# Window attention on one Trainium2 core: the table of offloaded score tiles planned anew, with no score tile computed twice

## The chip, the core and the metric

The kernel runs on one core of one Trainium2 chip. The core's engines run side by side and are tied together by semaphores: TensorE (PE, matmuls, with its weight loads shown apart as PEld), VectorE (DVE), ScalarE (ACT), GpSimd (POOL) and SyncE (SP, which here only issues DMAs). The metric is the device time of one execution in microseconds (us). Matmul results land in PSUM, which the program divides into eight banks of 512 fp32 columns on 128 partitions; everything else of the working set lies in SBUF.

## The reference

An image of 224 x 224 positions with 96 channels (bf16) goes through cross-shaped window attention. Half of the channels attend inside horizontal stripes of 8 rows, the other half inside vertical stripes of 8 columns; a stripe has 8 x 224 = 1792 tokens, and there are 28 stripes of each direction.

```python
sw = 8; C2 = C // 2; nh, nw = H // sw, W // sw
qkv = einsum('bhwc,cd->bhwd', x, wqkv)
q, k, v = qkv[..., :C], qkv[..., C:2*C], qkv[..., 2*C:]
scale = C2 ** -0.5
# first 48 channels: stripes of 8 rows
qh, kh, vh = [t[..., :C2].reshape(B*nh, sw*W, C2) for t in (q, k, v)]
ah = softmax(einsum('bqc,bkc->bqk', qh, kh) * scale)
oh = einsum('bqk,bkc->bqc', ah, vh)
# last 48 channels: the same over stripes of 8 columns -> ov
o = concat(oh, ov)                      # per position
return einsum('bhwd,dc->bhwc', o, wo)
```

So each of the 56 stripes has a softmax over a 1792 x 1792 score matrix, and the exponentials of all of these, 56 x 1792 x 1792 = 180 million, are most of the elementwise work.

## The kernel before, in words

**Tiles.** Stripes go in 28 pairs P (14 pairs of row stripes, then 14 of column stripes); the two stripes of a pair sit in the two halves of the partitions. A pair's 1792 queries are cut into four chunks c of 512, 512, 512 and 256. A score tile is a key block of 128 keys against one chunk of 512 queries for both stripes: 128 partitions x 1024 fp32, two PSUM banks. (In the 256 chunk a tile takes two key blocks.) This gives 14 + 14 + 14 + 7 = 49 tiles a pair and 1372 in all.

**What happens to a tile.** PE computes the scores, an exponential is taken of all 128 x 1024, the result is written as bf16 into one of 16 buffers `PT`, and PE multiplies it with V (`pv_fn`, L696) into an accumulator bank. A row of ones in V gives the softmax's denominator. There are two kinds of tile:

- Kind "A": the scores (`qk_fn`, L670) go into bank pair 0/1, 2/3 or, when it is free, 6/7. ScalarE reads them there and takes the exponential (L888, one ACTIVATE a tile).
- Kind "P", off ScalarE: the scores (`s_fn`, L683, with one row more in the contraction, which adds a constant so that the bits of the fp32 word can be read as a power of two) always go into banks 6/7 (`PB0`). The exponential is built out of those bits: the upper half of the word gives the power of two, a parabola of the lower half corrects it. Three ways of doing this are in the code, and which one a tile takes is decided when its first VectorE step is planned:

```python
tl["whole"] = backlog(t) < 2.0 * how()[11]                                # L1189
tl["stay"] = not tl["whole"] and backlog(t) >= 2.0 * how()[12]             # L1190
```

`backlog` is the planned time of the work that waits for GpSimd, in us. The three ways are:

1. *Copied* (`whole`): VectorE copies the whole tile to a buffer `qb` (L1191) and the banks are free; GpSimd does the rest in four steps (L1108 to L1111).
2. *Made twice* (neither): VectorE takes the lower halves out with one pass (L1192) and the banks are free; GpSimd squares them (L1105); then PE computes the same scores again into banks 6/7 (a second `s_fn`), and VectorE joins both with one pass (L1213).
3. *Stays* (`stay`): VectorE does three passes (L1192, L1205, L1213) while the scores stay in banks 6/7.

**The planner.** The order of every engine's instructions is fixed when the program is built. A list scheduler (`Sched`, `step_pe`, `step_dve`, `step_pool`) steps through planned time with durations written in the file (L25 to L40) and takes for each engine the next piece of work; `settle` and `emit` then write each engine's stream with the semaphore waits. What the planner may choose is set by the table `HOW`, one row for each pair:

- a string of three digits: how many of the tiles of chunks 0, 1 and 2 are of kind "P" (`OFF`, L73; chunk 3 has none),
- `TAIL`: how late the next pair's projections are spread,
- four rules of 13 digits, one for each chunk (`RULES`, L75). Digits 0 to 5 are thresholds for when PE goes over to PV matmuls, how many tiles off ScalarE may be under way, and which bank is kept; 6 an order on VectorE; 7 whether kind "A" may use banks 6/7; 8 and 10 small time windows; 9 whether the last sum of an output group goes to GpSimd (L584) or stays on VectorE (L593); 11 and 12 the two thresholds quoted above.

**Around it.** PE also runs the projections of the next pairs (K L435 with eviction L440, Q L435 with L451, V L481 with L488) and the output projections (L530, L566, with L537, L545, L573, L580, L593), in four banks 4 to 7 that they share with the PV accumulators and the "P" tiles. Columns and transposes come by DMA from the SP queue. When the share of PE's matmuls in the last 3.4 us falls, the planner puts small matmuls on a buffer of zeros in (L1095). Each engine works strictly in the order of its stream.

Of the kernel before, what the change touches and what calls it, by code (L numbers as in the profile page):

```python
# [40 lines left out]


HOW = [
    ("013", 9, "4551280019333 2571180019333 2583180019323 4583180019323"),
    ("434", 9, "4583180029333 3994191014411 2642191020314 2642191020310"),
    ("444", 2, "2642191020241 2642191020242 2622191020232 2682191020233"),
    ("433", 2, "2682191020434 2682171020430 2682171005430 3682171035430"),
    ("334", 8, "3733151007440 3734151007442 5983170025134 3351190004341"),
    ("444", 9, "3353190009341 3353190009341 3212271001233 3212271101433"),
    ("433", 6, "3212271101433 3213171101433 3213171121433 4144251027212"),  # L50
    ("254", 6, "3982170130134 2191161009232 3774280007321 5774280007321"),
    ("323", 6, "3933181026442 5933181026242 5993181026242 5993181026242"),
    ("443", 7, "5993160026242 5913160025242 5913160025442 5613160025443"),
    ("344", 9, "3a73180118424 3a73180118440 3a73180138440 3a73181138440"),
    ("434", 2, "3a73181138420 3a73181034420 3a44360007332 2464141207431"),
    ("333", 12, "3994240136212 3943290210143 4583180234434 4724171025341"),
    ("433", 12, "4771171035341 3422181006331 4482181006331 4482181016331"),
    ("333", 8, "5024381000243 3021381030243 2832290100230 4743281017314"),
    ("444", 0, "4743250017314 2334371013432 2331371023432 2733371023422"),
    ("413", 8, "2731371023420 2731271023440 2731271023414 2732271020424"),  # L60
    ("444", 6, "3611271029414 3611271029434 3612271019434 3612271019432"),
    ("323", 10, "2a83291022413 2a83291002413 2a83291006443 2a83271006443"),
    ("345", 9, "2a83271036443 3a83271036443 5871260114024 2942340018221"),
    ("334", 1, "2942371018224 2942361018224 2474291006112 2474291006124"),
    ("333", 1, "2444291006444 2044291026444 3884140034313 3884290034313"),
    ("333", 9, "3884290024313 3881290024313 2183281019241 2183281239341"),
    ("434", 7, "4733270022423 4733270022423 4733151022423 4783151022433"),
    ("333", 5, "5443191025313 5643191125213 5644191025213 5434190106422"),
    ("444", 6, "2163161034424 2183161034424 2583161004421 2983161004420"),
    ("432", 2, "5844290117302 5844290117312 5844290127314 2844290127340"),  # L70
    ("444", 12, "2844290125340 2844290110340 3792181100323 3212370220212"),
]
OFF = [[int(d) for d in k] + [0] for k, _, _ in HOW]  # L73
TAIL = [t for _, t, _ in HOW]
# [1287 lines left out]
```

## Time and profile before

Three runs took 1017.83 us in the median (1017.16 to 1017.92). The profiled execution took 1017.39 us, with a span of 1015.6 us from its first to its last instruction.

| | busy, us | share of the span | instructions |
|---|---|---|---|
| PE (matmul) | 979.1 | 96% | 13404 |
| PEld (weight loads) | 394.3 | 39% | 13404 |
| DVE | 959.7 | 94% | 1517 |
| ACT | 1004.8 | 99% | 1101 |
| POOL | 921.6 | 91% | 702 |

In rows of groups the columns are line, engine, operation, output <- inputs with shapes and count; then busy time in us, the mean of one in ns; then the idle time of that engine just before such instructions, and who ended it. The mean of one can be longer than its share of the busy time, because instructions of an engine overlap at their ends. Of the 1372 tiles ScalarE took 1090 and the other 282 went the three other ways: 136 copied (the count of L1191), 75 staying (that of L1205) and 71 made twice (that of L1105). The second scores of those 71 are in L683's count: 4 x (282 + 71) = 1412.

### The profile page before, as it was taken

The numbers are of one execution on the slowest core, as the hardware profiler recorded it, in microseconds if no ns is written. First come the engines' busy times: TensorE is split into PE (matmuls) and PEld (weight loads), VectorE is DVE, ScalarE is ACT, GpSimd is POOL, SyncE is SP. The second block draws the span as 40 slices with busy tenths as digits, with TensorE's granted clock in tenths as the row PEclk, the third lists the DMA queues.
The fourth block names the chain that finished last, engine by engine and source line by source line (L and its number), as shares of the span: only waits on it lengthen the run. The fifth ranks groups of instructions, "written<-read, shape, count | busy, mean of one in ns | idle before, by whom it ended". The sixth has DMA issues, their size and how long they took to land.

```text
span 1015.6 us, 30858 instructions
## 1 busy us (share of the span) xinstructions
PE 979.1 (96%) x13404; PEld 394.3 (39%) x13404; DVE 959.7 (94%) x1517; ACT 1004.8 (99%) x1101; POOL 921.6 (91%) x702
## 2 busy tenths in 40 slices
PE   9999999999999999999999999999999999999998
PEld 4433433343343333334333433434343333443333
DVE  7999999999999999999999999999999999999997
ACT  8999999999999999999999999999999999999997
POOL 4988999999988999989999999989989999998895
PEclk9999999999999999999999999999999999999999
DMA  4402112303220311211022033213313321221111
GB/s 87 98 29 65 38 42 66 65 2 79 65 38 29 79 38 30 65 38 39 2 39 50 19 65 62 49 23 64 48 25 60 57 43 36 58 54 22 25 26 34
DMA packets 162875, 47.04 MB, mean 46 GB/s; under 512 B 155895, under 2 KB 162711, under 8 KB 162738
## 3 DMA queue, kind: packets, MB, share of 16 engines
q1 hardware_dynamic: 161906, 44.62, 21.8%
q8 instruction: 105, 1.72, 0.7%
q10 hardware_dynamic: 832, 0.44, 0.2%
q14 instruction: 32, 0.26, 0.1%
HBM read 10.60 MB, written 19.28 MB: 29 GB/s over the span
## 4 chain that ended last, share of the span: by engine, by line
ACT 97%; PE 2%; DVE 1%; issue 0%; DVEq 0%; ACTq 0%
ACT PT L888 97%; PE ps L696 0%; PE ps L346 0%; PE ps L670 0%; DVE out_all L593 0%; DVE PT L1213 0%; ACT xT_sb L747 0%; PE ps L731 0%; PE ps L566 0%; DVE rc L573 0%; DVE OT_sb L1166 0%; PE ps L481 0%; DVE warm L309 0%; PE ps L683 0%; DVEq L192 0%
## 5 line engine op out<-in xcount | busy, mean ns | idle before, releaser
L888 ACT ACTIVATE PT<-ps 128x1024 bf16<-128x1024 f32 x1090 | 1000.4, 1092 | 1.2 <-PE ps L670 1.1
L670 PE MATMUL ps<-QT_sb,KT_sb 49*64 49x512 bf16 (+1 forms) x5144 | 447.7, 363 | 28.5 <-ACT PT L888 12.4
L696 PE MATMUL ps<-PT,V_sb 128*49 128x512 bf16 (+1 forms) x3136 | 456.2, 361 | 0.7 <-ACT PT L888 0.5
L670 PEld LDWEIGHTS ps<-QT_sb,KT_sb 49*64 49x64 bf16 x5144 | 130.1, 103 | 366.9 <-ACT PT L888 351.0
L1109 POOL TENSOR_TENSOR PT<-PT 128x1024 f16<-128x1024 f16 x136 | 257.6, 1894 | 10.1
L696 PEld LDWEIGHTS ps<-PT,V_sb 128*49 128x49 bf16 x3136 | 133.9, 103 | 165.2 <-issue 129.4
L1110 POOL TENSOR_SCALAR qb<-PT 128x1024 uint16<-128x1024 f16 x136 | 183.7, 1350 | 11.8
L1192 DVE TENSOR_SCALAR qb<-ps 128x1024 f32<-128x1024 uint16 x146 | 178.3, 1221 | 7.5 <-PE ps L683 5.8
L1213 DVE SCALAR_TENSOR_TENSOR PT<-ps,PT 128x1024 uint16<-128x1024 bf16 x146 | 178.0, 1219 | 4.2 <-PE ps L683 3.7
L1108 POOL TENSOR_SCALAR PT<-qb 128x1024 f16<-128x1024 uint16 x136 | 142.4, 1047 | 41.7 <-DVE qb L1191 32.1
L1191 DVE COPY qb<-ps 128x1024 f32<-128x1024 f32 x136 | 166.2, 1222 | 8.6 <-PE ps L683 7.1
L1111 POOL TENSOR_SCALAR PT<-qb 128x1024 uint16<-128x1024 f32 x136 | 142.4, 1047 | 11.0
L683 PE MATMUL ps<-QT_sb,KT_sb 50*64 50x512 bf16 x1412 | 139.5, 385 | 1.9 <-DVE PT L1213 0.4
L1105 POOL TENSOR_TENSOR PT<-qb 128x1024 f16<-128x1024 f32 x71 | 133.1, 1894 | 1.1 <-DVE qb L1192 0.3
L1205 DVE SCALAR_TENSOR_TENSOR PT<-ps,qb 128x1024 f16<-128x1024 uint16 x75 | 91.4, 1219 | 0.2
L1166 DVE CAST OT_sb<-ps 113x512 bf16<-113x512 f32 x112 | 69.3, 619 | 7.1 <-PE ps L696 5.7
L451 DVE CAST QT_sb<-ps 128x512 bf16<-128x512 f32 (+1 forms) x111 | 68.0, 616 | 5.7 <-PE ps L435 5.1
L440 DVE TENSOR_SCALAR_CACHE_REDUCE KT_sb<-ps 128x512 bf16<-128x512 f32 x108 | 66.5, 616 | 1.0 <-PE ps L435 0.7
L584 POOL TENSOR_TENSOR out_all<-tmp,Ph_sb 128x480 bf16<-128x480 f32 (+1 forms) x57 | 59.2, 1046 | 2.6 <-DVE tmp L580 1.4
L488 DVE CAST V_sb<-ps 128x480 bf16<-128x480 f32 (+1 forms) x84 | 52.0, 621 | 4.6 <-PE ps L481 4.3
L545 DVE TENSOR_TENSOR Ph_sb<-ps,rc 128x480 bf16<-128x480 f32 (+1 forms) x84 | 52.2, 621 | 2.0
L683 PEld LDWEIGHTS ps<-QT_sb,KT_sb 50*64 50x64 bf16 x1412 | 40.1, 103 | 34.5 <-DVE PT L1213 13.0
(64 smaller groups left out, 458.1 us busy)
## 6 DMA issues: line engine op xcount, KB each, us to landing
cols_dram<-in_x_dram SPq DMA_DIRECT2D x28, 336.0 KB
out_dram<-out_all SPq DMA_DIRECT2D x388, 24.0 KB, 1.9
xT_sb<-cols_dram SPq DMA_TRANSPOSE x28, 4.7
xT_sb<-in_x_dram SPq DMA_TRANSPOSE x26, 4.5
xT_sb<-ones_dram SPq DMA_DIRECT2D x26, 7.0 KB
Ph_sb<-in_x_dram SPq DMA_DIRECT2D x2, 168.0 KB, 3.5
Ph_sb<-in_x_dram ACTq DMA_DIRECT2D x2, 168.0 KB, 3.7
out_dram<-out_all ACTq DMA_DIRECT2D x4, 24.0 KB, 2.4
```

The lines of the kernel that those rows point to most:

```text
L670: ins = e.matmul(bank(SETS[s] + w)[64 * kh:64 * kh + 64, i * t["qs"]:(i + 1) * t["qs"]], lhsT=KT_sb[b][64 * w:64 * w + CA, kt * 128 + 64 * ...
L683: ins = e.matmul(bank(PB0 + w)[64 * kh:64 * kh + 64, 0:512], lhsT=KT_sb[b][64 * w:64 * w + nr, kt * 128 + 64 * kh:kt * 128 + 64 * kh + 64] ...
L696: ins = e.matmul(bank(pb)[64 * w:64 * w + CA, 0:t["qs"]], lhsT=V_sb[b][:, w, kt, :], rhs=PT[slot][:, ca:ca + t["qs"]], start=st and i == 0 ...
L888: S.commit("act", 0.0, D_ACT, None, lambda e, s=s, slot=slot: e.activation(PT[slot][:], ps[:, 512 * SETS[s]:512 * SETS[s] + 1024], ACTF.Ex ...
L1105: return [("pool", (D_SQ, L_SQ, 0.0), lambda e: e.tensor_tensor(y, q, q, ALU.mult), qk, yk)]
L1108: return [("pool", (D_TS, L_TS, LATE_TS), lambda e: e.tensor_scalar(y, lo, 2.0 ** -16, QH, ALU.mult, ALU.add), qk, yk), ("pool", (D_SQ, L_ ...
L1109: ("pool", (D_SQ, L_SQ, 0.0), lambda e: e.tensor_tensor(y, y, y, ALU.mult), yk + ["pser"], yk),
L1110: ("pool", (D_TW, L_TW, LATE_TS), lambda e: e.tensor_scalar(lo, y, 65536.0 * P2, 65536.0 * QC0, ALU.mult, ALU.add), yk + ["pser"], [("q", ...
L1111: ("pool", (D_TS, L_TS, LATE_TS), lambda e: e.tensor_scalar(bits, q, 1.0, 128.0 * (127.0 - SOFF), ALU.mult, ALU.add), qk, yk)]
L1191: S.commit("dve", t, D_P1, D_P1 + SEMD, lambda e: e.tensor_copy(qb[tl["qb"]][:], ps[:, PB0 * 512:(PB0 + 2) * 512]) if tl["whole"] else e.t ...
L1192: qb[tl["qb"]][:], ps[:, PB0 * 512:(PB0 + 2) * 512]) if tl["whole"] else e.tensor_scalar(
L1213: S.commit("dve", t, D_P1, D_P1 + SEMD, lambda e: e.scalar_tensor_tensor(PT[tl["slot"]][:].bitcast(U16), half(BF16, 1), 128.0 * (127.0 - S ...
```

## The change

Nothing but the table `HOW` is changed: every one of its 28 rows is new, so the number of offloaded tiles of each chunk, `TAIL` and all rules differ. The digit 12 of all 112 rules is now 0. As `backlog(t) >= 0` always holds, a tile that isn't copied stays; the way "made twice" stays in the code and is never taken. The table's off counts add up to 279, where they were 282. Announced split: 163 tiles are copied and 116 stay. The code that computes anything, the buffers, the planner and its durations are the same.

```diff
 HOW = [
-    ("013", 9, "4551280019333 2571180019333 2583180019323 4583180019323"),
-    ("434", 9, "4583180029333 3994191014411 2642191020314 2642191020310"),
...
-    ("432", 2, "5844290117302 5844290117312 5844290127314 2844290127340"),
-    ("444", 12, "2844290125340 2844290110340 3792181100323 3212370220212"),
+    ("022", 8, "4551131003130 2833380005450 2833370015440 2832370011440"),
+    ("444", 7, "2162370010440 2163370010440 2163370010440 2163270010440"),
...
+    ("333", 9, "5931160006230 5223291027430 5223291107430 5223291107430"),
+    ("534", 1, "5722351122030 5782351122030 4993250020220 4993250020220"),
 ]
```

Tiles off ScalarE by pair, 0 to 27, before: 4 11 12 10 10 12 10 11 8 11 11 11 9 10 9 12 8 12 8 12 10 9 9 11 9 12 9 12; and in the new table: 4 12 11 9 10 10 12 10 10 9 11 12 10 10 9 9 11 10 10 9 10 9 9 13 9 10 9 12. Averaged over the 112 rules, digit 11 (the threshold for copying) goes from 2.68 to 3.16, digit 9 from 4.79 to 5.26, digit 10 from 3.13 to 2.73 and digit 5 (tiles under way) from 7.51 to 7.09.

More of the change, by code (lines that the diff above doesn't have):

```diff
@@ L43 @@
 HOW = [
-    ("013", 9, "4551280019333 2571180019333 2583180019323 4583180019323"),
-    ("434", 9, "4583180029333 3994191014411 2642191020314 2642191020310"),
[L46 to L69, printed above, removed]
-    ("432", 2, "5844290117302 5844290117312 5844290127314 2844290127340"),
-    ("444", 12, "2844290125340 2844290110340 3792181100323 3212370220212"),
+    ("022", 8, "4551131003130 2833380005450 2833370015440 2832370011440"),
@@ new lines @@
+    ("444", 7, "2162370010440 2163370010440 2163370010440 2163270010440"),
+    ("344", 12, "2163270010450 2153270010450 3742381018120 3742381028220"),
+    ("333", 1, "2892291134440 2a92291104430 2a22291004430 2a22291014430"),
+    ("334", 9, "2313191038430 2313191038430 4653171020440 4653171000440"),
+    ("433", 9, "4a22241012350 4822261012350 4822261012330 4822261032340"),
+    ("444", 11, "2224270005340 2224370005140 3033181007130 3a33181007330"),
+    ("433", 2, "2934171033250 2931271033250 3033160105350 3033160106350"),
@@ new lines @@
+    ("334", 9, "2572151019130 2572291019130 2372291019330 2372291019030"),
+    ("333", 12, "2371291029030 2371291029030 3792161110340 5763170007410"),
+    ("434", 4, "5763170037430 5a63170037430 5a63170037430 5643160008050"),
+    ("444", 0, "5643160008150 5643160008130 5643160028130 5653160028110"),
+    ("433", 8, "5112140007230 5114140007230 2923160020440 2922160020440"),
+    ("334", 6, "2661370005430 2722271127130 2722271127130 2522171127130"),
+    ("333", 8, "3522171127130 3522171127130 3522171127110 3522271129410"),
@@ new lines @@
+    ("333", 9, "3822271128450 3812271128450 5684350205140 5951190007310"),
+    ("425", 7, "5951190107310 5953190107310 5953190107330 5953190007330"),
+    ("334", 10, "5953191007350 5953191007350 5463170017440 5963170017410"),
+    ("433", 5, "5963170017430 5964170037430 3182261023420 3182241023220"),
+    ("333", 10, "5424270006030 5424270006430 5424270036420 5324270036450"),
+    ("334", 8, "2324270036450 2324270036430 3984371107420 3164160014320"),
+    ("423", 9, "3134160014320 3634160014320 3034160014320 3034160034320"),
@@ L72 @@
+    ("333", 12, "3034160014320 2641381022310 2322281028440 2322280008440"),
+    ("445", 11, "4752391029120 4752290029120 4752290029120 3881151000120"),
+    ("333", 3, "3381151000440 3443191017330 3443191017330 3443190016330"),
+    ("352", 6, "3443190003330 2354360207140 3611281023230 5421360006420"),
+    ("333", 9, "5931160006230 5223291027430 5223291107430 5223291107430"),
+    ("534", 1, "5722351122030 5782351122030 4993250020220 4993250020220"),
 ]
```

## The prediction

> **What bounds the kernel now.** I read the page first: busy time of each engine, then the chain of work that ended last.
>
> ```profile
> span 1015.6 us, 30858 instructions
> PE 979.1 (96%) x13404; PEld 394.3 (39%) x13404; DVE 959.7 (94%) x1517; ACT 1004.8 (99%) x1101; POOL 921.6 (91%) x702
> ACT 97%; PE 2%; DVE 1%; issue 0%; DVEq 0%; ACTq 0%
> ```
>
> Four engines are above 90%, so busy shares alone don't name the bound; the chain does, with 97% on ScalarE. To see whether ScalarE ever rests, the view of busy time by stretches of 100 us (busy and count for PE, PEld, DVE, ACT, POOL, then TensorE clock, DMA share, GB/s) is next:
>
> ```profile
> 9.00:109.00 100.00, 97.13 (x1323) 38.42 (x1321) 94.82 (x144) 99.69 (x109) 81.21 (x63) 1.00 0.26 58
> 209.00:309.00 100.00, 97.30 (x1365) 38.92 (x1362) 97.05 (x143) 100.00 (x110) 91.62 (x68) 1.00 0.23 54
> 809.00:909.00 100.00, 97.51 (x1380) 39.97 (x1376) 94.14 (x159) 100.00 (x110) 95.53 (x70) 1.00 0.24 44
> sum 1000.00, PE 968.83 PEld 387.82 DVE 953.51 ACT 999.61 POOL 916.37; mean PE 96.88 PEld 38.78 DVE 95.35 ACT 99.96 POOL 91.64
> ```
>
> From 9 to 1009 us ScalarE is busy 999.61 of 1000 us. Nothing that makes another engine lighter can shorten this part; only fewer tiles on ScalarE can. The timeline of ScalarE gives the price of a tile (start, length of the merged run, count):
>
> ```profile
> 9.31 21.19 ACT L888 ACTIVATE PT<-ps 128x1024 bf16<-128x1024 f32 x23 [1.10 <-PE ps L670]
> 89.14 81.73 ACT L888 ACTIVATE PT<-ps 128x1024 bf16<-128x1024 f32 x89
> 1008.67 1.15 ACT L888 ACTIVATE PT<-ps 128x1024 bf16<-128x1024 f32 x1
> ```
>
> and the groups by line give counts and durations (busy us, mean ns):
>
> ```profile
> L888 ACT ACTIVATE PT<-ps 128x1024 bf16<-128x1024 f32 x1090 | 1000.4, 1092 | 1.2 <-PE ps L670 1.1
> L670 PE MATMUL ps<-QT_sb,KT_sb 49*64 49x512 bf16 (+1 forms) x5144 | 447.7, 363 | 28.5 <-ACT PT L888 12.4
> L683 PE MATMUL ps<-QT_sb,KT_sb 50*64 50x512 bf16 x1412 | 139.5, 385 | 1.9 <-DVE PT L1213 0.4
> L1191 DVE COPY qb<-ps 128x1024 f32<-128x1024 f32 x136 | 166.2, 1222 | 8.6 <-PE ps L683 7.1
> L1192 DVE TENSOR_SCALAR qb<-ps 128x1024 f32<-128x1024 uint16 x146 | 178.3, 1221 | 7.5 <-PE ps L683 5.8
> L1205 DVE SCALAR_TENSOR_TENSOR PT<-ps,qb 128x1024 f16<-128x1024 uint16 x75 | 91.4, 1219 | 0.2
> L1213 DVE SCALAR_TENSOR_TENSOR PT<-ps,PT 128x1024 uint16<-128x1024 bf16 x146 | 178.0, 1219 | 4.2 <-PE ps L683 3.7
> L1105 POOL TENSOR_TENSOR PT<-qb 128x1024 f16<-128x1024 f32 x71 | 133.1, 1894 | 1.1 <-DVE qb L1192 0.3
> L1108 POOL TENSOR_SCALAR PT<-qb 128x1024 f16<-128x1024 uint16 x136 | 142.4, 1047 | 41.7 <-DVE qb L1191 32.1 <-DVE rc L573 0.5
> L1109 POOL TENSOR_TENSOR PT<-PT 128x1024 f16<-128x1024 f16 x136 | 257.6, 1894 | 10.1
> L1110 POOL TENSOR_SCALAR qb<-PT 128x1024 uint16<-128x1024 f16 x136 | 183.7, 1350 | 11.8
> L1111 POOL TENSOR_SCALAR PT<-qb 128x1024 uint16<-128x1024 f32 x136 | 142.4, 1047 | 11.0
> L584 POOL TENSOR_TENSOR out_all<-tmp,Ph_sb 128x480 bf16<-128x480 f32 (+1 forms) x57 | 59.2, 1046 | 2.6 <-DVE tmp L580 1.4
> ```
>
> The run of 89 tiles is one without a stall: (81.73 - 1.09) / 88 = 0.9164 us a tile, the 1.09 being the mean length of the last. At this pace 1090 tiles take 1089 x 0.9164 + 1.15 = 999.1 us; in fact they go from 9.31 to 1008.67 + 1.15 = 1009.82, that is 1000.5. So all stalls of ScalarE between its first and its last tile come to 1.4 us, each so short that the overlap of neighbouring tiles hides most of it from the busy time. The span is a head of 9.3, 999.1 of tiles, 1.4 of stalls and a tail of 1015.6 - 1009.8 = 5.8 us.
>
> **The change part by part.** *ScalarE, +2.75 us on the path.* The table's counts add up to 279 tiles off ScalarE where they were 282, so L888 goes from 1090 to 1093: 3 x 0.9164 = 2.75. No other work covers it, since ScalarE has no rest to put it into.
>
> *TensorE, off the path.* Score tiles into banks 6/7 were 282 + 71 = 353, at four matmuls each the 1412 of L683. Now they are 279, that is 1116 matmuls: 296 fewer. L670 gets 3 x 4 = 12 more. At 139.5 / 1412 = 0.099 us each the 284 are 28.1 us of busy time. I take nothing for it: the waits by engine show what TensorE does with time that it has over.
>
> ```profile
> PEld ps L670 <- ACT PT L888: 351.0, 926, 0.8
> PEld ps L683 <- DVE PT L1213: 13.0, 50, 0.6
> POOL PT L1108 <- DVE qb L1191: 32.1, 21, 8.4
> ACT PT L888 <- PE ps L670: 1.1, 1, 1.1
> ```
>
> The weight loads of ScalarE's score tiles wait 926 times, 351 us in all, for ScalarE to free its banks, and the one wait of ScalarE for TensorE that is listed is that before its first tile. What TensorE saves lengthens the 351.
>
> *VectorE, +9.8 us.* Copies L1191 from 136 to 163: 27 x 1.222 = +33.0. L1192 from 146 to 116: 30 x 1.221 = -36.6. L1205 from 75 to 116: 41 x 1.219 = +50.0. L1213 from 146 to 116: -36.6. Busy time goes from 959.7 to 969.5, which is 95.2% of a span of 1018.4.
>
> *GpSimd, +9.6 us.* Four steps of a copied tile are 1.047 + 1.894 + 1.350 + 1.047 = 5.338; 27 x 5.338 = +144.1. The 71 squares of L1105 go: 71 x 1.894 = -134.5. From 921.6 to 931.2, 91.4%. Digit 9 may also move some sums of output groups to or from L584, at 1.05 us each; the direction of three or so would be hidden in this, and I cost it at nothing.
>
> Neither sum is on the path while ScalarE is fed: the cover is ScalarE's own 1002 us, and it is gone only where VectorE or GpSimd has no room in some stretch. VectorE was busy 97.05 of 100 us in one stretch above, and GpSimd 95.53 in another, with ScalarE at 100.00 in both; the new means of 95.2 and 91.4 lie under these.
>
> *Banks 6/7.* A tile made twice had the pair twice, each time for one pass of VectorE; a tile that stays has it once for three, 1.221 + 2 x 1.219 = 3.66 us and more if VectorE does other work between. What is queued behind it on those banks is the next offloaded tile and the projections' fills that use banks 6 and 7, and behind these on TensorE, whose stream is in order, the scores for ScalarE. This is where the new order could cost ScalarE something. The holding in sum is the 9.8 us more on VectorE, less the latency of 74 fills.
>
> *Stalls, 1.4 us before.* The trace can't show those of a new order. From below: none at all, -1.4. From above: VectorE can't be filled beyond its present 959.7 / 1015.6 = 94.5%, so that 969.5 takes 1025.9, +7.5 beyond the three tiles. The rows are much nearer to the lower end (the stretch with VectorE at 97.05% has ScalarE at 100.00). I scale the present stalls with VectorE's idle time, from 55.9 to 48.9: 1.4 x 55.9 / 48.9 = 1.6, so +0.2.
>
> *Head and tail, 0.* What runs before the first tile is written by hand, with no digit of the table in it. The end of the chain of waits:
>
> ```profile
> 1009.88 0.42 PE ps L696 x4
> 1010.32 0.44 DVE OT_sb L1166
> 1010.80 0.29 PE ps L566 x8
> 1011.12 0.24 DVE rc L573 x2
> 1011.87 0.45 DVE out_all L593 x2
> ```
>
> These follow ScalarE's last tile, one after the other, whatever the table says: PV, eviction, output projection, reciprocals, scaling, and the last DMA. VectorE work that the new order leaves for the end could stand ahead of them (one pass, +1.2), and a gap or two may close (-0.5).
>
> DMAs, their queues and their number stay; the moments at which SP issues them move with the order, with nothing on ScalarE's path waiting for them (no DMA among its waits).
>
> *Sum.* 9.3 + (1092 x 0.9164 + 1.15 = 1001.9) + 1.6 + 5.8 = 1018.6, against 1015.6: +2.95. The profiled execution took 1017.39, so its like would take 1020.3; the median of the runs, 1017.83, lies 0.44 above it, which gives **1020.8 us**, 0.29% slower. 0.2%, or 2.04 us, is about what a measurement of this kernel can tell from no change.
>
> [...]
>
> ```profile
> L1109 POOL TENSOR_TENSOR PT<-PT x136: 1891/1894/1896, 19.9 to 994.0; 128x1024 f16<-128x1024 f16 x136
> ```
>
> 136 instances within 5 ns of one another, though VectorE was busy 94% of the time and copied 136 times. [...]
>
> **The rivals.**
>
> *TensorE was the bound, faster.* The page has it busy 96%, and 284 matmuls at 0.099 us go: 1017.8 - 28.1 = 989.7. Against it: the 351 us of waits for ScalarE, and 1093 tiles at 0.9164 alone need 1001.7. It decides only if ScalarE's pace depended on TensorE's load, and the pace is the same to within a few ns over all ten stretches (109 or 110 tiles in each). [...]
>
> *The stalls go, no change.* A stall of ScalarE comes where TensorE is late with its scores; the chain shows such a place, between the two runs
>
> ```profile
> 9.31 443.52 ACT PT L888 x483
> 457.48 541.35 ACT PT L888 x590
> ```
>
> where for 4.6 us it goes over TensorE's matmuls. If 74 tiles less for TensorE end all of the 1.4, it is 1017.83 + 2.75 - 1.4 = 1019.2, within 0.2%. It decides when at least 0.7 of the 1.4 go (below 1019.87). For it: stalls are TensorE's, and TensorE gets lighter. Against: TensorE is late mostly because something ahead of it in its order waits for VectorE, and that gets heavier.
>
> *VectorE or GpSimd runs out of room, slower by more.* A stay of 3.66 us in banks 6/7 delays the fills behind it, or a stretch with many copies is late with its `PT`. By the share of 94.5% above: 1017.8 + 10.3 = 1028.1; a third of these stalls gives 1023.1. By GpSimd, 931.2 / 0.9075 is 1026.1 in span, the same. It decides when a stretch asks VectorE for more than the 97% seen. For it: 41 more stays, and GpSimd waits 32.1 us for copies already. Against: the means above.
>
> [...]
>
> *The split isn't 163 and 116.* The total of 279 is fixed by the table; each tile moved from copied to staying costs VectorE 2.44 and saves GpSimd 5.34, which ends in the third rival.
>
> **How the numbers follow.** Forecast (stalls of 0.8 to 3, 1020 to 1022.2): 0.62. Stalls go: 0.17. Out of room or another split: 0.17. TensorE the bound, or a faster ScalarE for a reason that I don't see: 0.03. Locking: 0.01. So faster 0.03; same 0.17 and a little of the forecast's lower edge, 0.19; slower 0.78. The range goes from 1018.9, which leaves out the faster cases and some of the second (stalls gone and a shorter tail), to 1024.2, which takes in the third up to stalls of 5 us.
>
> **What the new profile would show.** L888 x1093 with 1003 us busy, and ScalarE at 99.9 of 100 us in the stretches; no L1105; L1191 x163; L1192, L1205 and L1213 x116; L683 x1116; DVE near 969.5, POOL near 931; the wait of L670's weight loads for ScalarE above 351. The prediction is wrong if ScalarE shows idle time before L888 of several us, if its first tile isn't at 9.3, or if more than 6 us or less than 5 follow its last.

## The result, and the profile after

The changed kernel took 1019.99 us in the median of 12 runs (1019.26 to 1021.12), the kernel before 1017.52 in 12 runs beside them (1016.52 to 1018.35). The ratio is 1.0025 with a 95% interval of 1.0017 to 1.0033: 2.5 us slower. The forecast was 1020.8, with 1018.9 to 1024.2 as its range. The profiled execution took 1019.99, with a span of 1018.2; that of before had 1017.39 and 1015.6, so both rose by 2.6.

The page's first part, and the chain of work that ended last:

```profile
span 1018.2 us, 30267 instructions
PE 964.7 (95%) x13117; PEld 385.9 (38%) x13117; DVE 964.2 (95%) x1534; ACT 1007.7 (99%) x1104; POOL 931.6 (91%) x736
ACT 82%; POOL 13%; PE 3%; DVE 1%; issue 1%; DVEq 0%
```

The groups by line (busy us, mean ns, then idle time before them):

```profile
L888 ACT ACTIVATE PT<-ps 128x1024 bf16<-128x1024 f32 x1093 | 1003.3, 1096 | 1.5 <-PE ps L670 1.3
L1109 POOL TENSOR_TENSOR PT<-PT 128x1024 f16<-128x1024 f16 x163 | 308.8, 1894 | 12.6
L1110 POOL TENSOR_SCALAR qb<-PT 128x1024 uint16<-128x1024 f16 x163 | 220.1, 1350 | 14.2
L1191 DVE COPY qb<-ps 128x1024 f32<-128x1024 f32 x163 | 199.2, 1222 | 12.2 <-PE ps L683 10.5
L1108 POOL TENSOR_SCALAR PT<-qb 128x1024 f16<-128x1024 uint16 x163 | 170.7, 1047 | 30.9 <-DVE qb L1191 17.8
L1111 POOL TENSOR_SCALAR PT<-qb 128x1024 uint16<-128x1024 f32 x163 | 170.7, 1047 | 13.1
L1205 DVE SCALAR_TENSOR_TENSOR PT<-ps,qb 128x1024 f16<-128x1024 uint16 x116 | 141.3, 1218 | 0.1
L683 PE MATMUL ps<-QT_sb,KT_sb 50*64 50x512 bf16 x1116 | 111.2, 387 | 4.2 <-DVE PT L1213 1.9
```

All counts are as announced: 1093 tiles on ScalarE, 163 copied, 116 staying, no L1105, and 1116 score matmuls off ScalarE. What is new is the chain: 13% of it lies on GpSimd, which wasn't in it before. Its pieces in order of time (start, length), at the place where it leaves GpSimd ("issue" is time in which GpSimd waited for nothing that the profile shows; four such pieces of 0.04 to 0.07 us are left out here):

```profile
420.00 1.06 POOL PT L1108
421.13 1.06 POOL PT L1111
422.26 1.90 POOL PT L1109
424.16 0.08 issue
424.24 1.34 POOL qb L1110
425.58 0.08 issue
425.66 1.06 POOL PT L1108
426.79 1.06 POOL PT L1111
427.89 0.83 PE ps L696 x6
428.72 0.37 PE ps L670 x4
```

From 312.4 to 427.9 us the chain stays on GpSimd, which does one copied tile after another without a pause; a tile takes 425.66 - 420.00 = 5.66 us, of which 5.34 is busy and the rest is 0.07 to 0.08 us between the steps. In fact GpSimd has no pause of 0.3 us or more from 18.9 to 534 us; in the kernel before it had ten in that time, 14 us in all. At the end of the stretch PV (L696) waits for the last step, and the scores for ScalarE stand behind PV in TensorE's order. The timelines of TensorE and ScalarE there:

```profile
427.89 0.34 PEld L696 LDWEIGHTS ps<-PT,V_sb 128*49 128x49 bf16 x6 [0.69 <-POOL PT L1111]
429.11 1.94 ACT L888 ACTIVATE PT<-ps 128x1024 bf16<-128x1024 f32 x2 [0.24 <-PE ps L670]
```

This is ScalarE's longest idle time in mid-kernel. There are two more: 0.12 us at 491.0, where a second such stretch of GpSimd in the chain ends (465.3 to 490.2), and 0.06 at 742.5. The end of the kernel, first ScalarE's last piece in the chain and then the last of the tail:

```profile
1004.83 8.26 ACT PT L888 x9
1013.13 0.42 PE ps L696 x4
1013.58 0.44 DVE OT_sb L1166
1015.13 0.45 DVE out_all L593 x2
```

ScalarE's busy time by stretches sums to 999.26 of 1000 us, as good as before:

```profile
sum 1000.00, PE 951.93 PEld 377.99 DVE 955.38 ACT 999.26 POOL 926.32; mean PE 95.19 PEld 37.80 DVE 95.54 ACT 99.93 POOL 92.63
```

ScalarE's last tile ends at 1013.09. Its first starts at 9.31 as before; 1093 tiles at 0.9164 us end at 9.31 + 1092 x 0.9164 + 1.15 = 1011.2, so its stalls came to 1.9 us, and the tail is 1018.2 - 1013.1 = 5.1. Against the kernel before: +2.75 of tiles, +0.5 of stalls, -0.7 of tail, together +2.6 (the first two are counted at the pace of the kernel before, 0.9164).

### The profile page after: what moved, and what is told of

Read it like the earlier page. It is cut to its first block, busy times and chain, and to the rows that moved or that the text cites. A ratio compares the mean times of both kernels' runs of the same rounds, so it can differ in the third digit from the quotient of the medians.

```text
span 1018.2 us, 30267 instructions
## 1 busy us (share of the span) xinstructions
PE 964.7 (95%) x13117; PEld 385.9 (38%) x13117; DVE 964.2 (95%) x1534; ACT 1007.7 (99%) x1104; POOL 931.6 (91%) x736
## 4 chain that ended last, share of the span: by engine, by line
ACT 82%; POOL 13%; PE 3%; DVE 1%; issue 1%; DVEq 0%
ACT PT L888 82%; POOL PT L1109 4%; POOL qb L1110 3%; POOL PT L1108 3%; POOL PT L1111 3%; PE ps L696 1%; PE ps L670 1%; PE ps L346 0%; DVE qb L1192 0%; DVE qb L1191 0%; DVE PT L1205 0%; ACT xT_sb L747 0%; DVE Ph_sb L545 0%; PE ps L731 0%; DVE OT_sb L1166 0%
## 5 line engine op out<-in xcount | busy, mean ns | idle before, releaser
L670 PE MATMUL ps<-QT_sb,KT_sb 49*64 49x512 bf16 (+1 forms) x5156 | 448.5, 363 | 42.7 <-ACT PT L888 29.9
L696 PE MATMUL ps<-PT,V_sb 128*49 128x512 bf16 (+1 forms) x3136 | 452.2, 361 | 0.9 <-POOL PT L1111 0.4
L1109 POOL TENSOR_TENSOR PT<-PT 128x1024 f16<-128x1024 f16 x163 | 308.8, 1894 | 12.6
L670 PEld LDWEIGHTS ps<-QT_sb,KT_sb 49*64 49x64 bf16 x5156 | 130.2, 103 | 377.8 <-ACT PT L888 363.4
L1110 POOL TENSOR_SCALAR qb<-PT 128x1024 uint16<-128x1024 f16 x163 | 220.1, 1350 | 14.2
L1191 DVE COPY qb<-ps 128x1024 f32<-128x1024 f32 x163 | 199.2, 1222 | 12.2 <-PE ps L683 10.5
L1108 POOL TENSOR_SCALAR PT<-qb 128x1024 f16<-128x1024 uint16 x163 | 170.7, 1047 | 30.9 <-DVE qb L1191 17.8
L696 PEld LDWEIGHTS ps<-PT,V_sb 128*49 128x49 bf16 x3136 | 133.2, 103 | 166.1 <-issue 128.3
L1111 POOL TENSOR_SCALAR PT<-qb 128x1024 uint16<-128x1024 f32 x163 | 170.7, 1047 | 13.1
L1192 DVE TENSOR_SCALAR qb<-ps 128x1024 f32<-128x1024 uint16 x116 | 141.8, 1222 | 8.1 <-PE ps L683 7.1
L1213 DVE SCALAR_TENSOR_TENSOR PT<-ps,PT 128x1024 uint16<-128x1024 bf16 x116 | 141.4, 1219 | 0.3
L1205 DVE SCALAR_TENSOR_TENSOR PT<-ps,qb 128x1024 f16<-128x1024 uint16 x116 | 141.3, 1218 | 0.1
L683 PE MATMUL ps<-QT_sb,KT_sb 50*64 50x512 bf16 x1116 | 111.2, 387 | 4.2 <-DVE PT L1213 1.9
L683 PEld LDWEIGHTS ps<-QT_sb,KT_sb 50*64 50x64 bf16 x1116 | 32.0, 104 | 34.3 <-DVE PT L1213 15.2
L481 PEld LDWEIGHTS ps<-w_sb,xT_sb 96*64 96x64 bf16 x1568 | 37.6, 112 | 9.8 <-issue 1.5
```

What stands on the lines that cost most here:

```text
L670: ins = e.matmul(bank(SETS[s] + w)[64 * kh:64 * kh + 64, i * t["qs"]:(i + 1) * t["qs"]], lhsT=KT_sb[b][64 * w:64 * w + CA, kt * 128 + 64 * ...
L683: ins = e.matmul(bank(PB0 + w)[64 * kh:64 * kh + 64, 0:512], lhsT=KT_sb[b][64 * w:64 * w + nr, kt * 128 + 64 * kh:kt * 128 + 64 * kh + 64] ...
L696: ins = e.matmul(bank(pb)[64 * w:64 * w + CA, 0:t["qs"]], lhsT=V_sb[b][:, w, kt, :], rhs=PT[slot][:, ca:ca + t["qs"]], start=st and i == 0 ...
L1108: return [("pool", (D_TS, L_TS, LATE_TS), lambda e: e.tensor_scalar(y, lo, 2.0 ** -16, QH, ALU.mult, ALU.add), qk, yk), ("pool", (D_SQ, L_ ...
L1109: ("pool", (D_SQ, L_SQ, 0.0), lambda e: e.tensor_tensor(y, y, y, ALU.mult), yk + ["pser"], yk),
L1110: ("pool", (D_TW, L_TW, LATE_TS), lambda e: e.tensor_scalar(lo, y, 65536.0 * P2, 65536.0 * QC0, ALU.mult, ALU.add), yk + ["pser"], [("q", ...
```

## The experiments

The theory under test: three tiles more on ScalarE, which has no rest, are the difference. The rivals: stalls that the new order makes by GpSimd or VectorE, and TensorE's load. Each kernel was timed against the kernel before, on the same chip; the kernel before took 1017.1 to 1017.5 in each of these sets, so that gains against the changed kernel, which compare two sets, are good to a few tenths of a microsecond. Except for the last, every edit is made where the instructions are issued and leaves the planned durations alone, so the order of all engines is that of the changed kernel (or of the kernel before, where said).

**TensorE's part alone, on the kernel before.**

```diff
-                S.commit("pe", t1, D_MM, L_PV, s_fn(tl, 50), kt_keys(tl), PBK, fresh=PBK,
+                S.commit("pe", t1, D_MM, L_PV, s_fn(tl, 50, 512 if k == "s1" else 64), kt_keys(tl), PBK, fresh=PBK,
```

> The kernel before in its own order, but the second making of the 71 tiles' scores writes 64 of each 512 columns (the rest of the banks keeps what was there, so those tiles' values are not the scores). This takes TensorE's part of what the change removes off the kernel before, and nothing else. Theory: TensorE waits 351 us for ScalarE, so nothing is gained: 1017.5 within 0.5 us. Rival (TensorE's work is on the path): 71 x 4 matmuls at 0.099 us, 28 us of busy time, show as a gain of several us.

1017.05 us, ratio 0.9998 (0.9988 to 1.0007). The edit took 13.5 us off L683's busy time (139.5 to 126.0), about half of the 28.3 that the change takes off it, since a matmul of 64 columns still took some 0.05 us, by these sums, where one of 512 took 0.099. That half is worth nothing that can be measured, and the changed kernel, with 14.4 us less of TensorE, isn't faster either; that rival falls. ScalarE's stalls, by the count above, are 1.4 us as before, so the rival that a lighter TensorE ends them falls with it.

**A few of ScalarE's tiles cut short.**

```diff
+            n = 64 if ia[0] in range(250, 1150, 300) else 1024
-                PT[slot][:], ps[:, 512 * SETS[s]:512 * SETS[s] + 1024], ACTF.Exp, scale=LN2 / 128.0),
+                PT[slot][:, 0:n], ps[:, 512 * SETS[s]:512 * SETS[s] + n], ACTF.Exp, scale=LN2 / 128.0),
```

> The changed kernel in the same order, but three of ScalarE's tiles in mid-kernel take the exponential of 64 of their 1024 columns (the rest of the tile is left as the buffer held it). One ACTIVATE of 512 columns took 0.58 us and those of 1024 took 1.09, so each cut saves some 0.8 to 0.9 us of ScalarE. Theory (ScalarE's count of tiles sets the time): three tiles are the whole difference, so the time falls by about 2.5 us from 1020.0 to the time of the kernel before, 1017.5. Rival (the difference comes from stalls that the new order makes, by VectorE or GpSimd): it stays at 1020 within 0.5 us, since the stalls remain and fill up what is cut.

1020.06 us, ratio 1.0033 (1.0020 to 1.0046). No gain: the number was the rival's. With twelve tiles (`range(120, 1080, 80)`) and with 48 (`range(110, 1070, 20)`):

> The same with twelve tiles cut, 80 tiles apart. Theory: 12 x 0.8 = 9.6 us less than the changed kernel, about 1010.4. Rival (VectorE at 95% and GpSimd at 91% are as near to the bound as ScalarE): the other engines come to bind, and well under half of it is gained, 1016 or more.

1019.39 us, ratio 1.0022 (1.0013 to 1.0032), a gain of at most 0.6, hardly clear of the noise, where 9.6 were expected.

> The same with 48 tiles cut, 20 tiles apart. Theory, if nothing else bound: 48 x 0.8 = 38 us less, 982. VectorE's busy time of 964 and GpSimd's of 932 leave room for at most 1018 - 964 = 54 us by VectorE, so I expect a part of it to be lost, 985 to 1000. Rival: not under 1010.

1017.13 us, ratio 0.9998 (0.9988 to 1.0009), 2.9 us where I expected 20 to 35 and the rival had at most 10. The timeline of ScalarE in the kernel with three cut tiles shows why:

```profile
237.75 1.27 ACT L889 ACTIVATE PT<-ps 128x1024 bf16<-128x1024 f32 x2
239.61 1.02 ACT L889 ACTIVATE PT<-ps 128x1024 bf16<-128x1024 f32 x1 [0.58 <-PE ps L670]
```

The second of the two tiles is the cut one; it ends at 239.02, some 0.8 us early, and the next starts at 239.61 all the same, because it has to wait 0.58 for its scores. TensorE's work before them goes on as it did:

```profile
238.38 0.83 PE L696 MATMUL ps<-PT,V_sb 128*49 128x512 bf16 x6
239.15 0.11 PEld L670 LDWEIGHTS ps<-QT_sb,KT_sb 49*64 49x64 bf16 x4 [0.42 <-ACT PT L889]
```

and in the changed kernel:

```profile
238.49 0.83 PE L696 MATMUL ps<-PT,V_sb 128*49 128x512 bf16 x6
239.25 0.11 PEld L670 LDWEIGHTS ps<-QT_sb,KT_sb 49*64 49x64 bf16 x4 [0.42 <-ACT PT L888]
```

Three PV tiles stand between one score fill and the next. All of this is 0.10 to 0.11 us earlier than in the changed kernel, but so it was before the cut tile: from the start of the cut tile to that of the next are 0.95 us in both. A tile shortened by itself gains what TensorE has left in that one round, here nothing, and 0.05 to 0.06 us a tile in the runs with twelve and 48. So these three runs say nothing on what a tile costs when it is taken out of the plan together with its scores: the test was wrong, not yet the theory. A saving has to be spread so thinly that it stays below TensorE's slack in each round.

**The same saving spread over all tiles.**

```diff
+            n = 1024 if ia[0] < 60 else 1021
```

> The changed kernel in the same order; every tile of ScalarE from the 60th on leaves out the last 3 of its 1024 columns. The runs before showed that a single tile cut short only makes ScalarE wait for the next scores, since TensorE's work between two score fills is fixed; spread thin, each saving of 2.5 ns lies well under the 0.39 us that the score fills wait for ScalarE on average. Theory (ScalarE's sum of work sets the time): 1033 x 2.5 ns = 2.6 us less, about 1017.4, the time of the kernel before. Rival (the difference is stalls by VectorE and GpSimd): no change, 1020 within 0.5.

1018.63 us, ratio 1.0014 (1.0005 to 1.0024): half of what the theory said came, 1.4 of 2.6 us, more than the rival's nothing. (The intervals of this kernel and of the changed one overlap; the runs hardly do, 1018.30 to 1019.49 in eleven against 1019.26 to 1021.12 in twelve.) With 1000 in place of 1021:

> The same with 24 of 1024 columns left out, 20 ns a tile, 20.7 us in all. Theory: if the other engines have the room that their idle time says (54 us VectorE, 87 us GpSimd), most of it shows, 1000 to 1004. Rival (the new order holds VectorE, GpSimd and TensorE as close as ScalarE): under a third of it, 1013 or more.

1013.38 us, ratio 0.9968 (0.9956 to 0.9980): 6.6 of 20.7 us, the rival's number. Three lines of ScalarE's timeline, the first two with waits that break it:

```profile
428.75 1.90 ACT L889 ACTIVATE PT<-ps 128x1000 bf16<-128x1000 f32 x2 [1.68 <-PE ps L670]
431.69 76.38 ACT L889 ACTIVATE PT<-ps 128x1000 bf16<-128x1000 f32 x84 [1.04 <-PE ps L670]
508.33 473.33 ACT L889 ACTIVATE PT<-ps 128x1000 bf16<-128x1000 f32 x524 [0.27 <-PE ps L670]
```

At 428.75, at the end of GpSimd's run without a pause, ScalarE waits 1.68 us, and soon after 1.04 more; from 508 on, 524 tiles go through with no idle time that shows (at 0.903 us each, they too are slower than the 0.9164 - 0.020 that the edit aims at). The second wait has another cause than the first. A row of TensorE's timeline, and the two stretches of 3.4 us there (busy times of PE, PEld, DVE, ACT and POOL, then the granted TensorE clock):

```profile
427.35 0.83 PE L696 MATMUL ps<-PT,V_sb 128*49 128x512 bf16 x6 [1.61 <-POOL PT L1112]
424.80:428.20 3.40, 1.48 (x18) 0.44 (x18) 2.52 (x4) 2.27 (x3) 3.16 (x4) 1.00 0.00 0
428.20:431.60 3.40, 3.40 (x44) 1.44 (x48) 2.17 (x3) 1.90 (x2) 3.23 (x3) 0.50 0.00 0
```

(L1112 here is L1111 of the other kernels, one line further down.) While PV waits 1.61 us for GpSimd, TensorE is busy for only 1.48 of 3.40 us, and for the next 3.40 us its granted clock is 0.50: a score fill of four matmuls takes 0.65 us in place of 0.41, and ScalarE waits again. So a late GpSimd was paid for twice here, with 1.68 and with 1.04 us of ScalarE's time. The busy times by stretches say the same of GpSimd (last of the five engines):

```profile
309.00:409.00 100.00, 95.10 (x1326) 38.58 (x1320) 94.55 (x140) 98.11 (x110) 94.27 (x71) 1.00 0.21 50
409.00:509.00 100.00, 95.37 (x1310) 38.81 (x1308) 93.65 (x142) 96.66 (x108) 93.83 (x71) 0.98 0.12 27
```

94.27 of 100 us looks like room. It is none: at 5.34 of 5.66 us a tile, 94.3% is what copied tiles without a pause fill.

**GpSimd or VectorE made lighter.**

```diff
-  e.tensor_scalar(lo, y, 65536.0 * P2, 65536.0 * QC0, ALU.mult, ALU.add), ...
+  e.tensor_scalar(lo[:, 0:512], y[:, 0:512], 65536.0 * P2, 65536.0 * QC0, ALU.mult, ALU.add), ...
```

> The changed kernel in the same order; the third GpSimd step of each of the 163 copied tiles (L1110, 1.35 us) does half of its columns (the parabola is left out of the other half), some 0.65 us less each, 106 us of GpSimd in all. In the profile of the changed kernel ScalarE's one idle gap in mid-kernel (0.24 us at 429.1) comes after a PV matmul that waited 0.7 us for GpSimd at the end of 20 copied tiles without a pause. Theory: that stall and a few like it go and nothing else, 0.3 to 1.0 us less, 1019.0 to 1019.7. Rival (GpSimd, with 13% of the chain, is the bound in those 130 us): at 106 / 1018 = 10% less work for it, ten per cent of the 130 us, over 5 us, is gained.

1019.25 us, ratio 1.0019 (1.0010 to 1.0028), in the middle of the theory's range. The step took 0.77 us in place of 1.35, 95 us less in all.

```profile
span 1017.3 us, 30267 instructions
ACT 99%; PE 1%; DVE 0%; issue 0%; DVEq 0%
ACT PT L888 <- PE ps L670: 1.1, 1, 1.1
```

GpSimd is out of the chain, ScalarE's only wait for scores is that before its first tile, and its stalls, by the same count as above, fall from 1.9 to 1.2. For VectorE, the pass of L1205 on half of its columns:

```diff
-   PT[tl["slot"]][:].bitcast(FP16), half(U16, 0), 1.0, qb[tl["qb"]][:], ALU.mult, ALU.mult),
+   PT[tl["slot"]][:].bitcast(FP16)[:, 0:512], half(U16, 0)[:, 0:512], 1.0, qb[tl["qb"]][:, 0:512], ALU.mult, ALU.mult),
```

> The changed kernel in the same order; the second VectorE pass of each of the 116 staying tiles (L1205, 1.22 us) does half of its columns (the other half of those tiles is not multiplied), some 0.53 us less each, 62 us of VectorE in all. Theory: VectorE is not on the path, a few tenths of the stalls go, 1019.0 to 1020. Rival (VectorE out of room at 95%): 62 / 964 of its share shows as several us, 1016 or less.

1019.50 us, ratio 1.0023 (1.0014 to 1.0032), as the theory said: 50 us less for VectorE (914.2 busy) and at most half a microsecond of gain. Neither is what makes the 2.5 us, though the intervals of these two and of the change itself overlap, so that the small gains are read from the traces.

**Both ScalarE and GpSimd lighter.** The edits of the spread columns, 3 and then 24, and of L1110 together:

> Both at once in the changed kernel's order: ScalarE's tiles leave out their last 3 columns from the 60th on (2.6 us in all) and L1110 does half of its columns. The 3 columns alone gave 1.4 of 2.6 us, and their trace has a stall of 0.7 us where GpSimd had run copied tiles without a pause. Theory (ScalarE's sum and GpSimd's full stretch bind side by side; with GpSimd lighter the columns count in full): 1019.25 - 2.6 = 1016.7, within 0.6. Rival (half is lost in the order anywhere, GpSimd or not): 1019.25 - 1.3 = 1018.0 or more.

1017.21 us, ratio 0.9999 (0.9990 to 1.0008). With GpSimd light, the 2.6 us taken off ScalarE give 1019.25 - 1017.21 = 2.0, and the kernel is as fast as the one before.

> 24 columns left out (20.7 us in all) and L1110 on half of its columns, same order. With the 24 columns alone ScalarE's tiles 300 to 500 took 92.7 and 93.5 us a hundred, no less than in the changed kernel, and the others 90.0 to 91.2 against 91.7 to 92.1. Theory: GpSimd's full stretch was what held them, and all hundreds now take 90.0 to 91.0: 1003 to 1006. Rival (TensorE's and VectorE's parts of the order hold them): 1010 or more.

1006.05 us, ratio 0.9890 (0.9877 to 0.9904), at the very edge of what the theory said: 13.2 us of 20.7 (against the run with L1110 halved), twice what came with GpSimd as it is. The stretches again:

```profile
309.00:409.00 100.00, 96.69 (x1332) 39.04 (x1332) 96.64 (x142) 99.89 (x112) 87.19 (x74) 1.00 0.22 50
409.00:509.00 100.00, 96.90 (x1346) 39.65 (x1344) 96.35 (x147) 99.77 (x111) 83.40 (x70) 1.00 0.15 31
```

ScalarE does 112 and 111 tiles there in place of 110 and 108, and the granted clock is 1.00 where the run with L1110 whole had 0.98. Of the 20.7 us 7.5 are still missing, though ScalarE shows as busy for 99.8 us and more in these stretches: its 1093 tiles stand in the timeline as one run without a stop, at 0.905 us each. TensorE and VectorE have 17% and 16% of that chain, GpSimd has none; that the 7.5 are theirs is argued from these shares and wasn't tried.

**The same columns off the kernel before.**

> The kernel before in its own order, with the last 24 of 1024 columns left out of ScalarE's tiles from the 60th on (1030 x 20 ns = 20.6 us). The changed kernel gave back 6.6 us for the same. Theory (GpSimd is what holds it; the kernel before gives GpSimd 136 copied tiles in place of 163, and the 71 squares between them leave it pauses): more than 9 us, 1004 to 1008.5. Rival (every order planned so tightly holds all engines alike): 5 to 8 us, 1009.5 to 1012.5.

1009.05 us, ratio 0.9918 (0.9903 to 0.9933): 8.3 us, between the two. The order before has GpSimd in 13% of its chain in this run too, so it isn't free of it, but it follows a lighter ScalarE somewhat further than the new one (6.6).

**The ban alone.** Digit 12 of all rules of the kernel before set to 0, nothing else; the planner plans anew:

```diff
-    ("013", 9, "4551280019333 2571180019333 2583180019323 4583180019323"),
+    ("013", 9, "4551280019330 2571180019330 2583180019320 4583180019320"),
...
```

> The kernel before with digit 12 of all 112 rules set to 0 and nothing else: the same 282 tiles off ScalarE and the same other rules, but no tile is made twice; what was made twice now stays or, as the waiting GpSimd work changes, is copied. The kernel's own planner puts the end of its last instruction at 1091 us, where it has 1016.3 for the kernel before and 1018.6 for the changed one. Theory (the rules hold only for the order that they were found with, so the change can't be split into the ban and the counts): 1085 to 1100. Rival (the ban alone costs little and the time goes by the count of ScalarE's tiles): 1016 to 1023.

1162.23 us, ratio 1.1425 (1.1392 to 1.1459). The planner copied 162 tiles and let 120 stay, nearly the split of the new table (163 and 116), so it isn't the split that costs. The change can't be divided into the ban and the counts: rules that were found with 71 tiles made twice stall ScalarE for 123 us without them.

```profile
L888 ACT ACTIVATE PT<-ps 128x1024 bf16<-128x1024 f32 x1090 | 1015.4, 1082 | 124.1 <-PE ps L670 122.8
L696 PE MATMUL ps<-PT,V_sb 128*49 128x512 bf16 (+1 forms) x3136 | 481.6, 389 | 12.4 <-POOL PT L1111 12.4
```

It also came out 70 us above the planned 1091, which had been right to 0.7 us for the two tuned tables (1016.3 and 1018.6 for spans of 1015.6 and 1018.2). Its mean granted TensorE clock is 0.899, where the profiled execution of every other kernel had 0.998 or more:

```profile
209.00:309.00 100.00, 90.10 (x1200) 35.14 (x1196) 85.64 (x127) 88.91 (x97) 84.82 (x65) 0.93 0.19 46
809.00:909.00 100.00, 94.88 (x998) 30.84 (x998) 76.75 (x119) 80.64 (x85) 68.45 (x55) 0.76 0.22 43
```

The granted clock is 0.93 in the first of these stretches and 0.76 in the second. TensorE's busy share doesn't show why: it is higher in the second (94.88 us against 90.10), with fewer matmuls (998 against 1200), so that one took 0.095 us on average in place of 0.075. Shorter stretches of the same run show what came before one such time:

```profile
230.10:233.50 3.40, 0.90 (x10) 0.22 (x6) 2.85 (x4) 0.74 (x1) 3.23 (x3) 1.00 0.00 0
233.50:247.10 13.60, 11.01 (x100) 4.21 (x104) 8.52 (x11) 6.03 (x6) 12.14 (x11) 0.50 0.01 2
```

TensorE is busy for 0.90 of 3.40 us, and then its granted clock is 0.50 for 13.60 us; in the run with 24 columns left out it was busy for 1.48 of 3.40 us before 3.40 us at 0.50. If the clock had only the two values that these short stretches show, 1.00 and 0.50, a mean of 0.899 says that it was at half for some 235 of the 1161 us (an estimate from this mean). That the clock makes up the 70 us is argued, not shown.

## Why the prediction was right, point by point

*ScalarE never rests, +2.75.* The sum of the span holds to 0.4 us (+2.95 forecast, +2.6 measured), with 3 x 0.9164 of tiles and ScalarE 999.3 of 1000 us busy again. The forecast of 1020.8 lay 0.8 above the median; 0.3 of this is its base, 1017.83 in three runs and 1017.52 in twelve. That it came so close is in part luck: stalls and tail were off by +0.3 and -0.7 and partly cancel. As a statement of cause it was too simple: it said that nothing but fewer tiles on ScalarE can shorten the middle of the kernel, and halving L1110, on GpSimd, shortened it by some 0.7 us. The spread columns show that ScalarE's work counts nearly in full (2.0 of 2.6 us) only where GpSimd isn't full, and about half (1.4 of 2.6) in the order as it is. Two engines bind side by side. That the count of tiles gives the time all the same, because the table was planned so that both just fit, is argued; the direct test, three tiles' worth of work more on ScalarE in the order before, wasn't made.

*TensorE, nothing.* Right, and shown on the kernel before for about half of it. The wait of L670's weight loads for ScalarE rose from 351 to 363 us:

```profile
PEld ps L670 <- ACT PT L888: 363.4, 934, 0.8
POOL PT L1108 <- DVE qb L1191: 17.8, 9, 8.4
```

*VectorE, +9.8.* The four groups rose by that (from 613.9 to 623.7), but the engine's busy time by 4.5 only, 964.2 where 969.5 was forecast: the groups of all of VectorE's lines sum to 1039.6 us before and to 1049.7 now, 79.9 and 85.5 more than its busy time, since instructions that follow one another closely overlap at their ends in these traces, and the overlap is counted once. The sum of the group times was an upper bound here. The forecast's ceiling for VectorE, 94.5%, was none: it is at 94.7% now, and at 97.1% in the fullest stretch with ScalarE at 100.00.

*GpSimd, +9.6.* Busy time rose by 10.0, as forecast, and the step failed all the same. It took GpSimd's 95.53 of 100 us in one stretch before for room, where GpSimd had a single pause, of 0.47 us (ScalarE wasn't held up there). Each step of a copied tile has some 0.08 us before it that isn't busy time (L1109, L1110 and L1111: 12.6 + 14.2 + 13.1 us for 163 tiles, three of the four gaps), so the 27 tiles cost 27 x 5.66 = 152.8 and the sum is about +18, not +9.6; and from 312 to 428 us GpSimd had no pause at all. Had I timed a copied tile by the spacing of its starts (5.66 us) and not by its busy time (5.34), the step would have come out at about +18.

*Stalls, +0.2.* They rose by 0.5. That the forecast was near is luck: it scaled them with VectorE's idle time, and those that the runs show come with GpSimd. The third rival, work that is late on VectorE or GpSimd, was there in small: GpSimd's stretch costs 0.7 us of stalls, by the run with L1110 halved. The second rival, that a lighter TensorE ends the stalls, fell.

*Head and tail, 0.* The head is the same; the tail is 5.1 us and not 5.8, just above the 5 that I had named as the limit. The steps from ScalarE's last tile to the last scaling take 2.5 us in both (to 1012.32 before, to 1015.58 now). What is shorter lies behind them, in the queues that issue the last output DMAs. Their timelines, SP and then ScalarE's queue, of the kernel before

```profile
1007.77 6.05 SPq L272 DMA_DIRECT2D out_dram<-out_all  x8
1009.20 3.67 ACTq L272 DMA_DIRECT2D out_dram<-out_all  x3
```

and of the changed one:

```profile
1007.11 9.31 SPq L272 DMA_DIRECT2D out_dram<-out_all  x13
1012.02 4.11 ACTq L272 DMA_DIRECT2D out_dram<-out_all  x5
```

SP issues without a pause at the end of both, one DMA in 0.76 us before (6.05 / 8) and in 0.72 now (9.31 / 13). It is through at 1007.77 + 6.05 = 1013.82 before, 1.5 us after the last scaling, and now at 1016.42, 0.8 after it; from there to the end of the span are 1.76 us in both. The new order has one DMA more of its last outputs on ScalarE's queue (5 against 4), and one issue of SP is about what the tail lost. The prediction passed over these queues with a sentence; this part wasn't tried by itself.

*Locking, 0.01.* No run shows this term: beside the 163 copies of VectorE, L1108 ran 1.047 to 1.048 us and L1109 1.892 to 1.897 us in all of their 163 instances.

## What to carry to other kernels

Where an order is planned so that several engines just fit, as here, the count of the units on the fullest engine times its pace can give the difference between two such orders; it gave none for the order that wasn't tuned (1162 us), and easing that engine alone doesn't give the same amount back. Judge an engine's room by the spacing of its starts in its fullest stretch, not by its mean busy share. And when a saving is to be measured on a pipeline with two buffers, spread it over all rounds: a tile that ended 0.8 us early in one round gained nothing here, as the next waited 0.58 us for its scores.

## What the runs showed of the hardware that I had not expected

GpSimd left 0.07 to 0.09 us between the steps of copied tiles that followed one another, so that back-to-back copied tiles showed as 94.3% busy (5.34 of 5.66 us). It wasn't so for all its work: before the 71 squares of L1105 in the kernel before, the idle time came to 1.1 us in all.

Two pauses of TensorE were followed by half of its clock. After stretches of 3.40 us with 0.90 us of matmuls (the ban alone) and 1.48 us (24 columns left out) the granted clock was 0.50 for 13.60 and 3.40 us; in the second case a score fill took 0.65 us in place of 0.41. In the badly ordered plan the granted clock was 0.76 in a stretch of 100 us and 0.90 over the whole, while in the profiled executions of all tuned orders the mean stayed at 0.998 or above.
